# mLSTM cell and squared-ReLU FFN on one core: another order for the main loop's transfers and for the vector work of the first FFN groups

## The chip, the cores and the metric

The kernel runs on one NeuronCore of one Trainium2 chip. The metric is the device time of one launch in microseconds (us); lower is better. PE is the matrix engine (PEld its weight loads), DVE the vector engine, ACT the scalar engine, POOL the GpSimd engine. SP issues nearly all DMAs, strictly in program order: an issue whose wait is not over holds up everything behind it.

## The reference

The first half is an mLSTM cell: batch 4, 8 heads, 768 steps, head size 40. The second half treats its output as 3072 rows of 320 and puts them through a feed-forward network with a squared ReLU.

```python
for t in range(S):
    m_new = np.maximum(f_gate[:, :, t] + m, i_gate[:, :, t])
    f_stab = np.exp(f_gate[:, :, t] + m - m_new)
    i_stab = np.exp(i_gate[:, :, t] - m_new)
    m = m_new
    C = f_stab[:, :, None, None] * C + i_stab[:, :, None, None] * np.einsum('bhd,bhe->bhde', vt, kt)
    n = f_stab[:, :, None] * n + i_stab[:, :, None] * kt
    h_tilde = np.einsum('bhde,bhe->bhd', C, qt)
    nq = np.einsum('bhd,bhd->bh', n, qt)[:, :, None]
    denom = np.maximum(np.abs(nq), 1.0)
    o = 1.0 / (1.0 + np.exp(-o_gate[:, :, t]))
    y[:, :, t] = o * h_tilde / denom
x = y.transpose(0, 2, 1, 3).reshape(3072, 320)
h = np.maximum(x @ w_in, 0.0)          # w_in: 320 x 2048
return h * h @ w_out                   # w_out: 2048 x 320
```

## The kernel before

**Tiling.** The rows are cut into 24 tiles of 128 (tile s: batch s // 6, chunk s % 6). The mLSTM cell is done chunk by chunk: within a chunk as masked scores (`scores`, `weighted`), between chunks through a state C that is decayed and added to. Two tiles make one of 12 FFN groups g. `ffn1_main` and `ffn1_rest` multiply by w_in in four parts per group, `relu_half` (ACT) takes the product out of PSUM (tile h_ps) into r_sb, `square_half` (DVE) squares it into g2. `ffn2_fast` multiplies by w_out in four steps per group, by a scheme with seven products instead of eight for a 2 by 2 block product; `sums` are its DVE additions (tiles S, g), and its `add`s (L759, out of PSUM into y_sb) are DVE work too. y_sb has three buffers for two tiles a group, so one of the group's buffers was the previous group's y1 and is free when that store (L779) has landed.

**Order.** The schedule is written out by hand: each engine gets its instructions in program order and waits on semaphores for the others. So the place of a call in the source sets the place of each of its instructions in the queue of its engine, and of its DMAs in SP's queue.

**The first FFN groups (loop over u = 0 to 7).** Here w_in and w_out are still being fetched and brought to the format that they are used in, piece by piece: `Rounding.words` is two ACT instructions a piece (L195, L197), `Rounding.join` three DVE instructions (L206, L210, L211), one POOL add (L215) and the issue of a later piece's fetch; `step` does what is due of both. Pieces 0 to 9 are w_in. u even: `turn_rows` (PE transposes of a normalised tile, ACT copy), `scores`, a quarter of the FFN's first product, `weighted`, `mask` (POOL, L359) and `weigh` (ACT, L383) of the next tile. u odd: `attend` (PE; then L466 and L471 on DVE, L474 and L479 on POOL), `normalise`, `transposes` of the next tile, another quarter. `idle(n)` issues n bf16 products of zeros that nobody reads; it takes a buffer of the h_ps pool, which has three here, as has the pool of `transposes`, `scores` and `attend`. r_sb has four buffers.

**The main loop (`parts`).** From n = 8 on the groups run in periods of eight parts, r = n % 8: r 0 and 1 are steps 0 and 1 of `ffn2_fast(g)`, r 2 to 5 the four quarters of the first product of group g + 2, r 6 and 7 steps 2 and 3. With b = 7 + 2 * (n // 8), tiles b and b + 1 of the cell are done meanwhile. Data that must be turned goes through DRAM:

- `pair_up(s)` copies k and q of a tile, DRAM to DRAM, into kq_rows (L287, four issues); `load_squares(s)` reads them back as blocks of 32 by 32 into kqT (L309, four issues), and `turn_kq` (DVE, L316) transposes the blocks. Scores on PE (L424) read kqT.
- `store_num(s)` writes the numerators to num_rows (L557), `load_num(s)` reads them back turned (L562, four issues), and `normalise_turned(s)` (DVE, L574 to L583) makes x_sb.
- `store_rows(s)` writes x_sb to x_rows (L613), `load_rows(s)` reads it as blocks (L618, four issues), and `turn_squares(s)` (DVE, L625) makes xT, which the first product (L649, L660) needs for both tiles of its group.

Each read back waits on SP until its write has landed. In a period SP's order is: at r 1 `load_rows(b - 1)`, `pair_up(b + 2)`; at r 2 `load_squares(b + 2)`; at r 3 `store_num(b)`, `load`, `load_num(b)`, `pair_up(b + 3)`; at r 4 `load_A`; at r 5 `store_rows(b)`, `store_num(b + 1)`, `load_rows(b)`, `load_num(b + 1)`; at r 6 y1's store (L779), `load`, `load_o`, `load_squares(b + 3)`; at r 7 y0's store (L784), `load_A`; at the next r 0 `store_rows` of the tile before.

Of the kernel before, what the change touches and what calls it, by code (L numbers as in the profile page):

```python
# [29 lines left out]
def kernel(  # L30
# [200 lines left out]
    rounding = Rounding()  # L231
# [86 lines left out]
    def load_o(s):  # L318
        b, c = divmod(s, NB)
        r, (s0, s1) = next((r, (a, z)) for r, (a, z) in enumerate(RUNS) if a <= s < z)  # L320
        if s == s0:
            st["og", r] = ld.tile([P, 4, H, D], F32, name="og")
        og = st.setdefault(s, {})["og"] = st["og", r][:, s - s0]
        nc.sync.dma_start(og, o_gate[b, :, c * P : (c + 1) * P, :].rearrange("h p d -> p h d"))

    def sigmoid(s):
        nc.scalar.activation(st[s]["og"], st[s]["og"], AF.Sigmoid)
# [28 lines left out]
    def mask(s):  # L356

        A = st[s]["A"][0]
        nc.gpsimd.affine_select(  # L359
            A[:], A[:], compare_op=ALU.is_ge, fill=-1e30, base=0, pattern=[[0, H], [1, P]], channel_multiplier=-1,  # L360
        )
# [55 lines left out]
    def scores(s, o=(False, False)):  # L417
        d = st[s]

        sc = [bank(o[i]) for i in range(2)]  # L420
        for j in range(PR):
            for i in range(2):
                rows = slice(DP * i, DP * i + D)
                nc.tensor.matmul(  # L424
                    sc[i][:, j, :], lhsT=d["kT"][rows, j, :], rhs=d["qT"][rows, j, :], start=True, stop=True,
                )
        d["sc"] = sc

    def weighted(s, spare=False):
        d = st[s]  # L430
        d["P"] = []
        for i in range(2):
            t = ffn.tile([P, W], F32, name="r_sb", bufs=4) if spare else work.tile([P, W], F32, name="P_sb")
            t = t[:].rearrange("p (j t) -> p j t", j=PR)
            d["P"].append(t)
            heads = slice(i, H, 2) if s < KQ_SQ else slice(PR * i, PR * (i + 1))
            nc.vector.tensor_tensor(t, d["sc"][i], d["W"][:, heads, :], op=ALU.mult)  # L437
# [185 lines left out]
    def turn_squares(s):  # L623
        t = st[s]["xT"]
        nc.vector.transpose(t, t)  # L625
        del st[s]
# [38 lines left out]
    def ffn1(g, pp):  # L665
        ffn1_main(g, pp)
        ffn1_rest(g, pp, st["half"][0])

    def relu_half():
        if "half" in st:  # L670
            hs, g4 = st.pop("half")
            rs = []
            for h in hs:
                rs.append(ffn.tile([P, 2, WG], F32, name="r_sb", bufs=4))
                nc.scalar.activation(rs[-1][:], h[:], AF.Relu)  # L675
            st.setdefault("relu", []).append((rs, g4))

    def square_half():
        if st.get("relu"):
            rs, g4 = st["relu"].pop(0)  # L680
            for i, r in enumerate(rs):
                nc.vector.tensor_tensor(g4[:, :, i, :], r[:], r[:], op=ALU.mult)  # L682
# [104 lines left out]
    def do(f, s):  # L787
        if 0 <= s < NT:
            f(s)
# [9 lines left out]
    def idle(n):  # L799
        t = ps_h.tile([P, W], F32, name="idle", tag="h_ps")  # L800
        for _ in range(n):
            nc.tensor.matmul(
                t[:], lhsT=zeros[:, :1].to_broadcast([P, P]), rhs=zeros[:, :1].to_broadcast([P, W]), start=True, stop=True,
            )
# [75 lines left out]
    for u in range(8):  # L880
        s = 2 + u // 2
        relu_half()
        if u % 2 == 0:
            if u == 0:
                ffn1(0, 0)
                scores(s)
                weighted(s)
                relu_half()
                rounding.step()
            else:  # L890
                if u == 2:
                    idle(4)
                turn_rows(s - 1)
                scores(s)
                ffn1(u // 4, u % 4)
            if u == 2:
                rounding.words()
            if u > 0:
                weighted(s)
            if u == 2:  # L900
                mask(s + 1)
                rounding.join()
                rounding.join()
                weigh(s + 1, masked=True)
                rounding.words()
            elif u == 0:
                rounding.words()
                weigh(s + 1, sums=False)
            else:
                weigh(s + 1)  # L910
                square_half()
        else:
            load_A(s + 2)
            for r in {1: (4,), 3: (5, 6), 5: (7,), 7: ()}[u]:
                load(r)
            if u == 5:
                for r in range(4, 8):
                    sigmoid(r)
            attend(s)
            if u == 3:  # L920
                square_half()
            sum_of_h(s)
            if u < 4:
                normalise(s)
            rounding.join()
            if u == 1:
                values(s + 1)
            if u > 4:
                normalise(s)
            for r in {5: (8,), 7: (9,)}.get(u, ()):  # L930
                load(r)
            for r in {5: (7,), 7: (8,)}.get(u, ()):
                pair_up(r)
            if u > 4:
                load_o(2 * s)
                load_o(2 * s + 1)
            transposes(s + 1)
            rounding.words()
            if u == 7:
                ffn1_main(1, 3)  # L940
                turn_rows(5)
                ffn1_rest(1, 3, st["half"][0])
                square_half()
                relu_half()
            else:
                ffn1(u // 4, u % 4)
                if u > 1:
                    square_half()
        if u < 4:
            load_o(4 + u)  # L950
        while rounding.done < NEXT[u]:
            rounding.step()
        if u == 1:
            square_half()
    square_half()
    load_A(8)
    load_squares(7)
# [44 lines left out]
    for n, (which, g, i) in enumerate(parts):  # L1002
        s, at = 6 + n // 4, n % 4

        r, b = (n % 8, 7 + 2 * (n // 8)) if n >= 8 else (None, None)
# [35 lines left out]

        if r == 0 and g > 1:
            sums(g, ALL, (3,))
        elif r == 1 and g > 2:
            do(turn_squares, b - 2)
        elif r == 4:
            do(scale_q, b + 1)
            do(turn_kq, b + 2)
        elif r == 5 and b > 9:
            do(normalise_turned, b)  # L1050
            do(store_rows, b)
        elif r == 7 and g < NG - 1:
            sums(g + 1, ALL, (2,))
# [57 lines left out]
        if r == 0 and g > 1:  # L1111
            do(decays, b + 1)
            do(mask, b + 1)
            square_half()
            do(normalise_turned, b - 1)
            do(store_rows, b - 1)
        elif r == 1:
            if g > 1:
                if g == 2:
                    turn_squares(9)  # L1120
                do(load_rows, b - 1)
                do(pair_up, b + 2)
            square_half()
            if g < NG:
                sums(g, ALL, (4,))
            do(scale_q, b)
            do(turn_kq, b + 1)
        elif r == 2:
            do(masked_W, b + 1)
            do(load_squares, b + 2)  # L1130
            if n == 10:
                load_rows(8)
        elif r == 3:
            do(decays, b + 2)
            do(mask, b + 2)
            attended(b)
            if b % 4 == 3:
                for t in range(b + 1, min(b + 5, NT)):
                    sigmoid(t)
        elif r == 4:  # L1140
            square_half()
            square_half()
            do(masked_W, b + 2)
            do(load_A, b + 3)
            if b > 9:
                do(turn_squares, b - 1)
        elif r == 5:
            do(store_num, b + 1)
            if b > 9:
                do(load_rows, b)  # L1150
                do(load_num, b + 1)
        elif r == 6 and b == 9:
            normalise_turned(9)
            store_rows(9)
            load_num(10)
            load_rows(9)
            load(14)
            turn_squares(8)
        elif r == 7 and b == 9:
            load_o(14)  # L1160
            load_o(15)
            load_squares(12)
            load_A(13)
        elif r == 6:
            do(load, b + 5)
            for t in range(b + 5, min(b + 7, NT)):
                load_o(t)
            do(load_squares, b + 3)
        elif r == 7:
            do(load_A, b + 4)  # L1170
# [35 lines left out]
```

## Time and profile before

| | |
|---|---|
| median of 12 runs | 524.98 us (521.52 to 527.21) |
| the profiled execution's own time | 526.89 us |
| its span, first to last instruction | 525.1 us |
| busy in the span: PE, DVE, ACT, POOL | 512.5, 333.0, 195.0, 88.2 us |
| mean granted clock of PE | 0.994 |
| moved by DMA | 68.06 MB, mean 130 GB/s |

How to read it: in the page's list of 40 slices each digit is the busy share of a slice in tenths; the row PEclk is the clock granted to PE in tenths. In a list of waits a line reads "engine, what waited, line <- what ended the wait: us in total, times, longest us". In a timeline a row is "start us, duration us, engine, line, operation, out<-in, shape, count", with the idle time before it in brackets; SPq rows are DMA issues. In a table of windows each engine has its busy time, then come the granted clock, the DMA share and GB/s.

### The profile page before, as it was taken

What the parts mean: (1) busy time and instruction counts of PE and PEld (TensorE: products, weight loads), DVE (VectorE), ACT (ScalarE), POOL (GpSimd) and SP (SyncE); (2) the same over time, 40 slices, a digit from 0 to 9 for tenths busy, and PEclk for the clock granted to TensorE, in tenths of its full rate; (3) what the DMA queues carried; (4) which work ended last, traced back from release to release, by engine and by line L of the source; (5) the groups of instructions that cost most, each with busy time, mean ns of one, the idle gap of its engine ahead of it and who ended that gap; (6) DMA issues with size and microseconds to landing.
All of it is one profiled execution on the core that took longest, in us unless ns stands there. A gap on an engine that the chain in (4) does not pass through costs nothing. (4 is left out here: it accounts for less than half of the span.)

```text
span 525.1 us, 10345 instructions
## 1 busy us (share of the span) xinstructions
PE 512.5 (98%) x3937; PEld 448.7 (85%) x3937; DVE 333.0 (63%) x638; ACT 195.0 (37%) x460; POOL 88.2 (17%) x110
## 2 busy tenths in 40 slices
PE   9998999999999999899999999989999999999997
PEld 4777888886798988798898898888898898998997
DVE  8479988868884772774774773664865864431451
ACT  3776568452645226232335424233532301102000
POOL 3255643222212010010110010010110100000000
PEclk9899899999999999999999999999999999999999
DMA  9998599876877775875784775775864221200000
GB/s 191 228 198 184 141 194 204 212 170 125 194 139 152 161 144 112 184 126 123 162 140 113 165 134 125 153 144 123 168 151 80 78 73 39 61 12 1 26 27 25
DMA packets 239394, 68.06 MB, mean 130 GB/s; under 512 B 185744, under 2 KB 233872, under 8 KB 239344
## 3 DMA queue, kind: packets, MB, share of 16 engines
q1 hardware_dynamic: 239248, 67.20, 60.6%
q8 instruction: 31, 0.51, 0.4%
q10 hardware_dynamic: 96, 0.20, 0.1%
q14 instruction: 19, 0.16, 0.1%
HBM read 55.08 MB, written 17.86 MB: 139 GB/s over the span
## 5 line engine op out<-in xcount | busy, mean ns | idle before, releaser
L649 PE MATMUL h_ps<-xT,w_in 128*128 128x256 f32 x768 | 174.1, 384 | 5.1 <-DVE xT L625 2.5
L649 PEld LDWEIGHTS h_ps<-xT,w_in 128*128 128x128 f32 x768 | 144.6, 191 | 28.0 <-DVE xT L625 3.4
L675 ACT ACTIVATE r_sb<-h_ps 128x512 f32<-128x512 f32 x96 | 51.4, 598 | 114.7 <-issue 51.5
L743 PE MATMUL h_ps<-w_out,g 128*128 128x160 f32 x528 | 75.5, 299 | 0.0
L682 DVE TENSOR_TENSOR g<-r_sb 128x512 f32<-128x512 f32 x96 | 67.4, 751 | 10.0 <-ACT r_sb L675 10.0
L743 PEld LDWEIGHTS h_ps<-w_out,g 128*128 128x128 f32 x528 | 72.9, 190 | 0.3 <-ACT W_sb L383 0.2
L383 ACT ACTIVATE W_sb<-A_bc,b_T 128x128 f32<-128x128 f32 x176 | 53.8, 388 | 23.4 <-POOL A_bc L359 23.2
L437 DVE TENSOR_TENSOR P_sb<-tp,W_sb 128x512 f32<-128x512 f32 x46 | 29.5, 683 | 44.7 <-PE numT L534 29.9
L743 PE MATMUL h_ps<-T,S 128*128 128x160 f32 x352 | 52.3, 302 | 0.0
L743 PEld LDWEIGHTS h_ps<-T,S 128*128 128x128 f32 x352 | 48.8, 190 | 1.6 <-issue 0.9
L660 PE MATMUL h_ps<-xT,w_in 64*128 64x256 f32 x384 | 49.0, 391 | 0.0
L660 PEld LDWEIGHTS h_ps<-xT,w_in 64*128 64x128 f32 x384 | 34.8, 186 | 12.1 <-issue 8.8
L763 ACT COPY y_sb<-h_ps 128x160 f32<-128x160 f32 x11 | 3.2, 293 | 95.9 <-PE h_ps L743 76.8
L316 DVE STREAM_TRANSPOSE kqT<-kqT 128x1024 f32<-128x1024 f32 x17 | 21.1, 1240 | 26.1 <-DMA kqT<-kq_rows 25.5
L359 POOL TENSOR_SCALAR_AFFINE_SELECT A_bc<-A_bc 128x1024 f32<-128x1024 f32 x22 | 25.4, 1153 | 68.8 <-ACT kq L369 56.7
L759 DVE TENSOR_TENSOR y_sb<-y_sb,h_ps 128x160 f32<-128x160 f32 x44 | 13.9, 315 | 36.0 <-PE h_ps L743 35.9
L396 POOL TENSOR_TENSOR vw<-va,W_sb 128x328 f32<-128x328 f32 x20 | 17.7, 886 | 69.4 <-ACT W_sb L383 50.3
L424 PEld LDWEIGHTS tp<-kqT 40*128 40x128 f32 x384 | 24.9, 188 | 4.8 <-issue 2.7
L490 POOL TENSOR_TENSOR Cd<-C,kq 128x164 f32<-128x164 f32 x15 | 7.0, 464 | 128.8 <-DVE C L551 106.5
L424 PE MATMUL tp<-kqT 40*128 40x128 f32 x384 | 26.5, 276 | 1.7 <-issue 1.2
L743 PE MATMUL h_ps<-w_out,S 128*128 128x160 f32 x176 | 26.0, 301 | 1.4 <-DVE y_sb L759 1.4
L369 ACT ACTIVATE kq<-A_bc 64x512 f32<-64x512 f32 x30 | 18.8, 628 | 21.4 <-DMA A_bc<-a_rows 19.6
(119 smaller groups left out, 602.3 us busy)
## 6 DMA issues: line engine op xcount, KB each, us to landing
A_bc<-a_rows SPq DMA_DIRECT2D x23, 512.0 KB, 5.1
raw<-in_moe_w_out_dram SPq DMA_DIRECT2D x16, 320.0 KB, 3.6
num_rows<-tn SPq DMA_DIRECT2D x18, 256.0 KB, 2.8
kq<-num_rows SPq DMA_DIRECT2D x72, 64.0 KB, 2.2
kqT<-kq_rows SPq DMA_DIRECT2D x34, 128.0 KB, 3.1
raw<-in_moe_w_in_dram SPq DMA_DIRECT2D x8, 512.0 KB, 4.8
kq<-in_k_dram SPq DMA_DIRECT2D x24, 160.0 KB, 4.0
va<-in_v_dram SPq DMA_DIRECT2D x24, 160.0 KB, 4.6
```

Of the source, the lines that this page charges most:

```text
L316: nc.vector.transpose(t, t)
L359: nc.gpsimd.affine_select(A[:], A[:], compare_op=ALU.is_ge, fill=-1e30, base=0, pattern=[[0, H], [1, P]], channel_multiplier=-1,)
L369: nc.scalar.activation(e[rows], st[s]["A"][0][rows, PR * i : PR * (i + 1), :], AF.Exp)
L383: nc.scalar.activation(d["W"][:, i * n + h, :], A[i][:, h, :], AF.Exp, bias=b_T[:, b, c, i * n + h : i * n + h + 1],)
L396: nc.gpsimd.tensor_tensor(d["vw"][:], d["va"][:], d["W"][:, :, P - 1 : P].to_broadcast([P, H, D1]), op=ALU.mult,)
L424: nc.tensor.matmul(sc[i][:, j, :], lhsT=d["kT"][rows, j, :], rhs=d["qT"][rows, j, :], start=True, stop=True,)
L437: nc.vector.tensor_tensor(t, d["sc"][i], d["W"][:, heads, :], op=ALU.mult)
L649: nc.tensor.matmul(hs[i][:, n, :], lhsT=w_in[:, a, fb * P : (fb + 1) * P], rhs=xT[:, :, a, :], start=(n == 0 and a == 0), stop=False,)
L660: nc.tensor.matmul(hs[i][:, n, :], lhsT=w_in2[rows, 2 * pp + n, :], rhs=xT[rows, :, 2, :], start=False, stop=(n == 1),)
L675: nc.scalar.activation(rs[-1][:], h[:], AF.Relu)
L682: nc.vector.tensor_tensor(g4[:, :, i, :], r[:], r[:], op=ALU.mult)
L743: nc.tensor.matmul(to, lhsT=lhsT[:, p], rhs=rhs[:, p, :], start=(start and p == 0), stop=(p == NPAIR - 1), skip_group_check=True,)
```

## The change

In the FFN loop, at u = 1 `relu_half` comes ahead of the steps of the rounding and the `square_half` behind them is left out there. At u = 2 the idle products go; `words`, the mask of the next tile and one `join` come ahead of `weighted`, and the left out `square_half` follows the second `join`. In the main loop `pair_up(b + 2)` goes ahead of `load_rows(b - 1)` at r 1, `load_num(b + 1)` moves from the end of r 5 to r 6, behind y1's store, and `turn_squares(9)` of the second period moves from behind step 1 of `ffn2_fast` to ahead of it.

```diff
             else:
-                if u == 2:
-                    idle(4)
                 turn_rows(s - 1)
                 scores(s)
                 ffn1(u // 4, u % 4)
             if u == 2:
                 rounding.words()
+                mask(s + 1)
+                rounding.join()
             if u > 0:
                 weighted(s)
             if u == 2:
-                mask(s + 1)
                 rounding.join()
-                rounding.join()
+                square_half()
                 weigh(s + 1, masked=True)
                 rounding.words()
...
             load_o(4 + u)
+        if u == 1:
+            relu_half()
         while rounding.done < NEXT[u]:
             rounding.step()
-        if u == 1:
-            square_half()
...
         if r == 0 and g > 1:
             sums(g, ALL, (3,))
-        elif r == 1 and g > 2:
+        elif r == 1 and g > 1:
             do(turn_squares, b - 2)
...
         elif r == 1:
             if g > 1:
-                if g == 2:
-                    turn_squares(9)
+                do(pair_up, b + 2)
                 do(load_rows, b - 1)
-                do(pair_up, b + 2)
             square_half()
...
             do(store_num, b + 1)
             if b > 9:
                 do(load_rows, b)
-                do(load_num, b + 1)
...
         elif r == 6:
+            do(load_num, b + 1)
             do(load, b + 5)
             for t in range(b + 5, min(b + 7, NT)):
                 load_o(t)
```

## The prediction

> **What bounds the kernel now.** I read the page first, then the waits of PE, then the timelines of SP and DVE around each wait.
>
> ```profile
> PE 512.5 (98%) x3937; PEld 448.7 (85%) x3937; DVE 333.0 (63%) x638; ACT 195.0 (37%) x460; POOL 88.2 (17%) x110
> PEclk9899899999999999999999999999999999999999
> ```
>
> PE is busy nearly throughout, and the chain of waits from 353.9 us to the end is PE alone. So only PE's gaps before that can be won, and whatever the change removes or adds there reaches the end undiluted. The waits of PE over 126 to 362 us (four lines), then over 42 to 76 us (two):
>
> ```profile
> PE h_ps L649 <- DVE xT L625: 2.5, 4, 0.9
> PE h_ps L743 <- DVE y_sb L759: 1.4, 3, 0.7
> PE tp L424 <- issue: 1.2, 1, 1.2
> PE tp L424 <- PE h_ps L660: 0.5, 1, 0.5
> ...
> PE h_ps L649 <- ACT r_sb L675: 1.4, 1, 1.4
> PE h_ps L649 <- POOL w_in L215: 0.2, 1, 0.2
> ```
>
> These idle numbers are low, because a modelled end hides part of a wait. I take start to start, against the same pair elsewhere in PE's timeline: L660 to L424 takes 1.84 us undisturbed (252.91 to 254.75), but 3.25 and 2.49 at 211.60 and 331.64. Product to product takes 2.17, but 2.86, 2.55 and 3.05 at 219.64, 259.94 and 338.92. The last product to L649 takes 4.35, but 5.41, 4.83, 4.93 and 5.34 at 187.54, 229.13, 308.06 and 348.59. What is lost: 1.41+0.65, then 0.69+0.38+0.88, then 1.06+0.48+0.58+0.99: 7.1 us in the main loop.
>
> Who causes them is read in SP's timeline (each row is a batch of issues):
>
> ```profile
> 197.87 0.52 SPq L613 DMA_DIRECT2D x_rows<-x_sb  x1
> 202.22 2.19 SPq L618 DMA_DIRECT2D xT<-x_rows  x4
> 204.45 1.79 SPq L287 DMA_DIRECT2D kq_rows<-in_k_dram  x2
> 206.29 1.23 SPq L287 DMA_DIRECT2D kq_rows<-in_q_dram  x2
> 208.63 2.48 SPq L309 DMA_DIRECT2D kqT<-kq_rows  x4
> 211.15 0.65 SPq L557 DMA_DIRECT2D num_rows<-tn  x1
> ...
> 224.17 1.87 SPq L618 DMA_DIRECT2D xT<-x_rows  x4
> 226.14 1.84 SPq L562 DMA_DIRECT2D kq<-num_rows  x4
> 228.07 0.38 SPq L779 DMA_DIRECT2D out_dram<-y_sb  x1
> ```
>
> From 198.39 to 202.22 SP stands still: load_rows (L618) waits for store_rows (L613) to land, and pair_up (L287) stands behind it though it waits for nothing. SP's waits total 27.3 us in nine such stops over 190 to 362 us. DVE shows who pays:
>
> ```profile
> 213.50 1.25 DVE L316 STREAM_TRANSPOSE kqT<-kqT 128x1024 f32<-128x1024 f32 x1 [7.28 <-DMA kqT<-kq_rows]
> 214.67 2.46 DVE L682 TENSOR_TENSOR g<-r_sb 128x512 f32<-128x512 f32 x4
> ...
> 230.17 0.33 DVE L759 TENSOR_TENSOR y_sb<-h_ps,y_sb 128x160 f32<-128x160 f32 x1 [3.66 <-DMA out_dram<-y_sb]
> ```
>
> **The change part by part.**
>
> **pair_up ahead of load_rows (r = 1).** Its four issues take 3.07 us (204.45 to 207.52) and move into the 3.83 us stop, so load_rows still goes out at 202.22. Its last copy would land about 2.4 us after its issue, near 203.9, so load_squares (L309) follows load_rows at 204.4 and not at 208.63: 4.2 us earlier. Its kqT buffer is free (last reader L485, done at 196.26). The squares then land near 209.2 instead of 213.38, and turn_kq (L316) ends near 210.4. The scores that PE wants at 213.44 no longer wait: 1.41 us, and in the same place three groups later 0.65. The four squares (L682) queued behind L316 end near 213, and with them ACT's wait for r_sb. store_num and load_num (landed 217.74) come 4.2 us earlier too, so normalise_turned moves forward, and the y_sb add that PE waits for at 222.50 is no longer at the end of one unbroken DVE run: 0.69 and 0.88. At 259.94 the wait hangs on load_num alone (DVE idles 1.77 us for it): 0.38.
>
> A rule that speaks against this: load_rows itself landed 2.25 to 3.2 us after issue. The Trainium skill, "DMA: Bandwidth & Descriptors", Queues, rings and completion order, has each DMA engine consume descriptors in ring order, so pair_up's data would go first. pair_up's landings are 2.0 us from first to last, so load_rows would land at 209.1 instead of 207.12. turn_squares wants it at 217.04, or about 213 after the change: still nothing lost; with that cover gone it would cost 2.0 us per group.
>
> **load_num behind y1's store (r = 5 to 6).** Four issues (1.84 us) and one store change places. DVE's add into y_sb stands at 230.17, 309.21 and 350.15 only because the old store has not landed; its product on PE ends at 229.3, 308.2 and 348.8. With the store 1.9 us sooner the add is bound by PE. From the add to the end of turn_squares DVE takes 3.73 us (230.17 to 233.90), so it ends at 233.0, 311.9 and 352.5, ahead of PE's need at 233.5, 312.4 and 352.9: 0.48+0.58+0.99. load_num goes 0.5 us later for the store; it landed at 229.51 and is asked for at 231.62, and the edit above brings it earlier. The new risk: SP now waits at L779 for y1's last add, with load_num, load and load_squares behind it. That add ended at 224.01, and SP gets there at 226.04: 2 us of cover, so nothing.
>
> **turn_squares(9) ahead.** One DVE transpose (0.57 us) passes one add. Its rows land at 192.14, PE waits until 192.95: it can gain 0.1 of the 1.06. The passed add is not waited for within 1 us.
>
> Main loop: 1.41+0.65+0.69+0.88+0.38+0.48+0.58+0.99+0.1 = 6.2 us at most. Part may return as another wait, as DMA times scatter: I take 5.6.
>
> **The FFN groups, u = 1 and 2.** idle(4), four bf16 products (1.04 us of PE at 48.09), goes, and relu (two ACT, 1.07 us) passes words, so h_ps is free at 50.1, not 52.3. It buys nothing: the third product instruction needs the weight piece whose join ends on POOL at 52.98, and PE in fact went on at 53.03. Nothing ahead of that join changes on DVE or POOL. The two words (1.2 us of ACT) that relu passes serve the next join, at 53.9.
>
> The waiting has a second price:
>
> ```profile
> 50.50:53.00 2.50, 0.91 (x4) 0.30 (x2) 2.47 (x3) 2.19 (x5) 1.85 (x2) 0.87 1.06 285
> 53.00:55.70 2.70, 2.67 (x6) 2.19 (x7) 2.67 (x4) 1.25 (x2) 1.57 (x2) 0.50 0.59 143
> ```
>
> The granted clock (third from last) is already 0.50 after a wait of 1.43 us. The Trainium skill, "TensorE: Matmul & The Clock Gate", What's actually happening, halves the clock only after an idle window of about 3.4 us and restores it after a busy one. By the rule the longer gap here (about 2.4 us in one piece) costs nothing and even today's slow stretch should not be there: a gain of 1.3. By the trace the slow stretch stays, and if its window is now not busy enough another of 3.4 us at half speed follows: 1.7 lost. I follow the trace and take the same stretch, 0.
>
> Then the order on DVE: now squares, weighted, join, join (53.90 to 61.46); afterwards join, weighted, join, squares. The instructions are the same, but an instruction that meets a running POOL operation stretches: L210 takes 1.37 us instead of 0.43, L211 1.11 instead of 0.69, a square 1.75 instead of 0.68. Today two meet one (+1.1, +0.9). Afterwards join 8 follows join 7 directly, so its L210 meets join 7's POOL add (+1.1) and its L211 the mask (+1.1), and the second square meets join 9's (+1.2): 1.3 us more. attend's L466 starts at 62.7 instead of 61.37; it frees the bank that PE's transposes take at 62.24, so PE waits until 63.2: 0.95. The relu of the third quarter waits for the squares (r_sb) until about 62.7, with 2 us of cover before PE needs that bank. The mask keeps its place on POOL, join's fetches go to SP some 1 us sooner. Later DVE is about 0.8 late against a PE that is 0.95 late: no more. No trace row shows this order: I bound it by -1.3 (clock kept) and +2.7 (both prices), and take +1.0.
>
> Sum: -5.6 + 1.0 = -4.6 us. The profiled execution took 526.89 us (span 525.1 and 1.8 around it): 522.3. It lies 1.9 above the median of the runs, 524.98, which I shift by the same: 520.4.
>
> **The rivals.**
>
> B, the DMA engines are the limit, not SP's order: earlier issues land no earlier. For it: a DMA share near 0.7 in the main loop, and store_rows taking 4 us to land behind a 512 KB load_A. Against it: the squares landed 2.4 to 2.7 us after issue, and SP stands idle. Half of 5.6 stays: -2.8+1.0, 523.2.
>
> C, the FFN groups cost both prices: -5.6+2.7, 522.1. For it, a DVE without idle from 47 to 74 us; against, that a slow PE hides the late DVE.
>
> D, slower: y1's store blocks SP. If DVE's last add of y1 ends after SP has reached L779, load_num waits. load_num takes 3.4 us from first issue to landing and is due about 1.6 us after the add at 229.3, so it hurts from a store later than 227.4 in this trace's time, and each us beyond is paid in six groups: from 1.1 us late (+6.6-5.6+1.0) it is slower, at 1.5 us late 529.4. Against: the add must come 4.5 us later than it does, and the 14.0 us that DVE now idles for the store says the store is what is late.
>
> E, the loop's edits do nothing, since the waits move to load_rows' own landing: only the FFN cost is left, 526.0.
>
> **How the numbers follow.** My forecast 0.68 (all faster), C 0.08 (0.07 faster, 0.01 same), B 0.11 (0.05 and 0.06), E 0.04 (same), D 0.09 (0.01 same, 0.08 slower). 0.3% (1.6 us) is about what a measurement of this kernel can tell from no change: limits 523.4 and 526.6. Faster 0.80, same 0.12, slower 0.08. My forecast's own ends are -6.2-1.3 and -4.5+1.7, that is 517.5 to 522.2; reaching into B for the rest, and leaving the extreme low end out, the range is 517.8 to 524.0.
>
> **What would show it.** Right: in SP's timeline L287 between L613 and L618; L309 some 4 us nearer to L613; L779 ahead of L562; DVE's 14.0 us for out_dram near 2; PE's waits for L759 and at L424 gone, one of about 0.8 for L625 left; near 62 us a new PE wait of 0.5 to 1.5 for DVE L466; the clock still near 0.5 for some 3 us after 53. Wrong: DVE's wait for kqT<-kq_rows as long as now (B), or SP waiting at L779 (D), or PE going on before 53.0.

## The result and the profile after

The changed kernel takes 520.65 us (median of 12 runs, 518.37 to 522.53) against 525.03 us (median of 49, among them those of the table above); the ratio is 0.9917, 95% interval 0.9894 to 0.994, so 4.4 us or 0.8% less. The profiled execution took 518.43 us with a span of 516.6 us, 8.5 us below the span before. That is more than the medians moved, because the two profiled executions lie on opposite sides of their medians. That of before was 1.9 us above: it had a stretch at half clock in its opening (14.8 to 18.2 us), and PE was already 1.9 us behind at the second quarter of the first group, where nothing had been changed yet. That of the changed kernel was 2.2 us below; what sets such executions apart is taken up with the last run. In the comparisons of profiles below, the start of L660 at the second quarter (47.03 us before, 45.17 after) is the zero.

Two lines of the page, then PE's waits over 120 to 355 us (three lines), then those over 42 to 76 us (one):

```profile
PE 508.1 (98%) x3933; PEld 447.2 (87%) x3933; DVE 336.1 (65%) x638; ACT 194.3 (38%) x460; POOL 90.9 (18%) x110
PEclk9999899999999999999999999999999999999999
```

```profile
PE h_ps L743 <- DVE S L738: 0.3, 1, 0.3
PE numT L534 <- DVE P_sb L437: 0.2, 1, 0.2
PE h_ps L649 <- DVE xT L625: 0.2, 1, 0.2
```

```profile
PE h_ps L649 <- POOL w_in L215: 2.6, 2, 2.2
```

All four kinds of wait in the main loop are gone; the 0.2 us for L625 that are left lie at 152 us, ahead of the periods that were edited. At the third quarter PE waits for POOL's add of the seventh weight piece in two pieces of 0.4 and 2.2 us, where it waited for ACT and POOL.

SP's timeline in the period that was shown of before:

```profile
196.65 0.74 SPq L613 DMA_DIRECT2D x_rows<-x_sb  x1
197.44 1.23 SPq L287 DMA_DIRECT2D kq_rows<-in_k_dram  x2
198.71 1.23 SPq L287 DMA_DIRECT2D kq_rows<-in_q_dram  x2
201.10 1.87 SPq L618 DMA_DIRECT2D xT<-x_rows  x4
203.08 3.40 SPq L309 DMA_DIRECT2D kqT<-kq_rows  x4
206.58 0.51 SPq L557 DMA_DIRECT2D num_rows<-tn  x1
...
219.50 1.86 SPq L618 DMA_DIRECT2D xT<-x_rows  x4
221.46 0.41 SPq L779 DMA_DIRECT2D out_dram<-y_sb  x1
221.97 1.82 SPq L562 DMA_DIRECT2D kq<-num_rows  x4
```

pair_up (L287) now fills the time in which store_rows (L613) lands. load_rows (L618) goes out 4.45 us after store_rows, as before (4.35). load_squares (L309) goes out 6.4 us after store_rows instead of 10.8, and y1's store (L779) stands ahead of load_num. DVE's answer:

```profile
209.05 1.25 DVE L316 STREAM_TRANSPOSE kqT<-kqT 128x1024 f32<-128x1024 f32 x1 [4.15 <-DMA kqT<-kq_rows]
210.22 3.00 DVE L682 TENSOR_TENSOR g<-r_sb 128x512 f32<-128x512 f32 x4
...
225.66 0.32 DVE L759 TENSOR_TENSOR y_sb<-h_ps,y_sb 128x160 f32<-128x160 f32 x1 [2.95 <-PE h_ps L743]
```

turn_kq ends at 210.30, 1.8 us before PE wants its scores (212.11), and the add into y_sb is released by PE's product and no longer by a store.

### The profile page after: what moved, and what is told of

It is laid out like the page before. It is cut to its first block, busy times and chain, and to the rows that moved or that the text cites. A ratio compares the mean times of both kernels' runs of the same rounds, so it can differ in the third digit from the quotient of the medians.

```text
span 516.6 us, 10360 instructions
## 1 busy us (share of the span) xinstructions
PE 508.1 (98%) x3933; PEld 447.2 (87%) x3933; DVE 336.1 (65%) x638; ACT 194.3 (38%) x460; POOL 90.9 (18%) x110
## 4 chain that ended last, share of the span: by engine, by line
PE 64%; DVE 0%; issue 0%
PE h_ps L743 29%; PE h_ps L649 22%; PE h_ps L660 6%; PE numT L534 2%; PE tp L424 2%; PE numT L523 1%; PE numT L512 1%; DVE S L738 0%; DVE y_sb L759 0%
## 5 line engine op out<-in xcount | busy, mean ns | idle before, releaser
L675 ACT ACTIVATE r_sb<-h_ps 128x512 f32<-128x512 f32 x96 | 50.3, 599 | 109.2 <-PE h_ps L660 62.5
L682 DVE TENSOR_TENSOR g<-r_sb 128x512 f32<-128x512 f32 x96 | 68.9, 767 | 10.1 <-ACT r_sb L675 10.0
L660 PE MATMUL h_ps<-xT,w_in 64*128 64x256 f32 x384 | 49.0, 391 | 0.0
L660 PEld LDWEIGHTS h_ps<-xT,w_in 64*128 64x128 f32 x384 | 34.8, 186 | 12.1 <-issue 9.1
L759 DVE TENSOR_TENSOR y_sb<-y_sb,h_ps 128x160 f32<-128x160 f32 x44 | 14.1, 320 | 43.5 <-PE h_ps L743 43.5
L359 POOL TENSOR_SCALAR_AFFINE_SELECT A_bc<-A_bc 128x1024 f32<-128x1024 f32 x22 | 26.9, 1221 | 68.2 <-ACT kq L369 53.5
L396 POOL TENSOR_TENSOR vw<-va,W_sb 128x328 f32<-128x328 f32 x20 | 19.1, 956 | 71.3 <-ACT W_sb L383 54.0
L424 PEld LDWEIGHTS tp<-kqT 40*128 40x128 f32 x384 | 24.8, 188 | 2.4 <-issue 0.9
L424 PE MATMUL tp<-kqT 40*128 40x128 f32 x384 | 26.1, 275 | 0.0
```

What stands on the lines that cost most here:

```text
L359: nc.gpsimd.affine_select(A[:], A[:], compare_op=ALU.is_ge, fill=-1e30, base=0, pattern=[[0, H], [1, P]], channel_multiplier=-1,)
L396: nc.gpsimd.tensor_tensor(d["vw"][:], d["va"][:], d["W"][:, :, P - 1 : P].to_broadcast([P, H, D1]), op=ALU.mult,)
L424: nc.tensor.matmul(sc[i][:, j, :], lhsT=d["kT"][rows, j, :], rhs=d["qT"][rows, j, :], start=True, stop=True,)
L660: nc.tensor.matmul(hs[i][:, n, :], lhsT=w_in2[rows, 2 * pp + n, :], rhs=xT[rows, :, 2, :], start=False, stop=(n == 1),)
```

## The experiments

Ratios are against the kernel before, measured beside it on the same chip, with 95% intervals.

**All three edits of the loop, first FFN groups as before.**

```diff
-        elif r == 1 and g > 2:
+        elif r == 1 and g > 1:
...
-                if g == 2:
-                    turn_squares(9)
+                do(pair_up, b + 2)
                 do(load_rows, b - 1)
-                do(pair_up, b + 2)
...
-                do(load_num, b + 1)
...
         elif r == 6:
+            do(load_num, b + 1)
```

> All three edits of the main loop, the first FFN groups as before. My theory (the loop's waits go, the FFN edits cost about 1 us): about 5.5 us below the kernel before, that is 1 us better than the full change; no PE wait of over 0.5 us between 185 and 355 us. Rival 1 (the FFN edits help, as they are meant to): less than the full change gains, at most 4 us below. Rival 2 (the DMA engines are the limit): at most 3 us below, with DVE's waits for kqT and for y_sb's store about as long as before.

Measured: 519.0 us against 525.42, ratio 0.9883 (0.9851 to 0.9916): 6.1 us less. PE's only wait in the loop is 0.2 us for P_sb. Both rivals fall: this is more than the full change gains, and the transfers that were issued earlier did land earlier. Over 120 to 372 us DVE's wait for kqT went from 25.5 to 11.1 us, and that for y_sb's store from 14.0 us to none.

**The FFN edits alone.** The diff is the other half of the change (relu, idle, words, mask, join, squares at u = 1 and 2).

> The edits at u = 1 and 2 alone, the main loop as before. My theory: 1.0 us slower than before (0 to 2.7): PE still goes on only when the POOL add of the seventh weight piece has ended, and then meets DVE 1 us late. Rival (relu was what PE waited for, and the idle products were dead weight): 1 to 2.5 us faster, with PE going on sooner after the second quarter than the 4.9 us that it takes now.

Measured: 526.92 us against 525.42, ratio 1.0035 (1.0015 to 1.0056): 1.8 us slower by the ratio, 1.5 by the medians. So the change is two changes of opposite sign, and -6.1 + 1.8 = -4.3 is the -4.4 of the whole. PE goes on 4.9 us after the end of the second quarter, as it did, so the rival falls.

**pair_up alone, and load_num alone.**

```diff
+                do(pair_up, b + 2)
                 do(load_rows, b - 1)
-                do(pair_up, b + 2)
```

> pair_up ahead of load_rows alone. My theory: the terms 1.41, 0.65, 0.69, 0.88 and 0.38 go, about 4.0 us less than before; the waits of PE for L625 stay (about 2 to 3 us), since y1's store is still behind load_num. Rival (pair_up's data ahead in the rings delays what follows): 1 us or less, with load_rows landing 2 us later than now and DVE's wait for kqT over 15 us.

```diff
-                do(load_num, b + 1)
...
         elif r == 6:
+            do(load_num, b + 1)
```

> load_num behind y1's store alone. My theory: the terms 0.48, 0.58 and 0.99 go, about 2.0 us less than before; DVE's 14 us of waiting for y_sb's store go to about 5 or less; the PE waits at L424 and for L759 stay. Rival (SP now stands at y1's store and load_num comes late instead): no gain or slower, with SP waiting at L779 and DVE waiting for num_rows.

Measured: pair_up alone 520.17 us, ratio 0.9909 (0.9875 to 0.9944), 4.8 us less; load_num alone 523.94 us, 0.9965 (0.9943 to 0.9987), 1.8 us less. PE's waits in the loop, first with pair_up alone (two lines), then with load_num alone (five):

```profile
PE h_ps L649 <- DVE xT L625: 0.9, 1, 0.9
PE numT L534 <- DVE P_sb L437: 0.2, 1, 0.2
```

```profile
PE tp L424 <- PE h_ps L660: 1.5, 2, 0.9
PE h_ps L743 <- DVE y_sb L759: 1.1, 2, 0.7
PE h_ps L649 <- DVE xT L625: 0.9, 1, 0.9
PE h_ps L743 <- ACT y_sb L763: 0.4, 1, 0.4
PE numT L534 <- DVE P_sb L437: 0.2, 1, 0.2
```

The second set is as expected, and DVE's wait for y_sb's store (14.0 us before) is gone with it. The first set is not: moving pair_up took away three of the four waits for L625 too, which I had given to load_num. With the queue some 4 us ahead, load_rows, load_num and y1's store all come early enough even in their old order: here the store is issued at 222.85, against 228.07 (4.0 us sooner, each counted from its zero, which is 45.83 here).

**pair_up and turn_squares(9), without load_num.** The first diff without its last two edits.

> pair_up ahead of load_rows and turn_squares(9) ahead, without the move of load_num, first FFN groups as before. From the profile of pair_up alone, in which PE's waits for L625 at the later groups were gone too: the same as all three edits of the loop, about 6.4 us less than before, so the move of load_num adds nothing where pair_up has moved. Rival (my forecast, which gave load_num's move 2.05 us of its own): about 4.5 us less than before.

Measured: 519.58 us against 525.52, ratio 0.9898 (0.9875 to 0.9921). By the interval both -6.4 and -4.6 us are possible, so times alone do not decide. In the profile the last two of PE's four waits for L625 are gone; at the first the rows were late, and at the second DVE's add still stood 4.9 us for the store (a line of DVE's waits over 120 to 372 us), and PE 1.0 us behind it:

```profile
DVE y_sb L759 <- DMA out_dram<-y_sb: 4.9, 1, 4.9
```

So load_num's move is a safeguard beside pair_up; its worth on average is too small for these intervals to show.

**turn_squares(9) alone.**

> turn_squares(9) ahead of step 1 of the second period alone. The forecast: 0.1 us, since the rows landed only at 192.14 us of the profile before. The other reading, from the profile after: behind the add of step 1, which needs that step's last product, the transpose can never be done before PE asks, so the edit is worth the whole 1.06 us wherever the rows have landed by then: about 1.0 us less, the PE wait for L625 near 192 us gone. Neither can show beyond the noise of a few runs, so the gap at that place in the profile decides.

Measured: ratio 0.9994 (0.9973 to 1.0014). In its profile, DVE's timeline near the place:

```profile
190.72 0.58 DVE L625 STREAM_TRANSPOSE xT<-xT 128x384 f32<-128x384 f32 x1 [0.45 <-DMA xT<-x_rows]
191.22 0.28 DVE L759 TENSOR_TENSOR y_sb<-y_sb,h_ps 128x160 f32<-128x160 f32 x1
```

The transpose passed the add, and then waited for its rows; PE still stood 0.76 us. Both readings hold, one after the other: the rows must have landed (in the full change, the loop's edits alone and, below, the run with DVE's old order they had, or nearly), and the transpose must not stand behind the add (with pair_up alone, 0.9 us were left).

**The idle products kept.**

```diff
             else:
+                if u == 2:
+                    idle(4)
                 turn_rows(s - 1)
```

> The full change, with the four idle products at u = 2 put back. My theory (PE waits there for the POOL add of the seventh weight piece and for nothing else): the same time as the full change within 0.3%, PE going on 4.9 us after the end of the second quarter as before. Rival 1 (removing them costs clock: the array cools down in the longer gap): about 0.5 to 1.7 us faster than the full change, clock above 0.8 in the 3 us after the gap. Rival 2 (they were dead weight): about 1 us slower than the full change.

Measured: 521.76 us, ratio 0.9931 (0.9905 to 0.9957) beside the full change's 0.9917 (0.9894 to 0.994): no difference that can be told. PE goes on 4.9 us after the end of the second quarter here too, so the products stood inside a wait.

**DVE's old order at u = 2, with the rest of the full change.**

```diff
             if u == 2:
                 rounding.words()
                 mask(s + 1)
-                rounding.join()
+                square_half()
             if u > 0:
                 weighted(s)
             if u == 2:
                 rounding.join()
-                square_half()
+                rounding.join()
```

> The full change, but with DVE's old order at u = 2: squares, weighted, join, join (relu ahead and no idle products stay). My theory (the FFN edits cost because DVE reaches attend's L466 about 1 us later): about 1 us faster than the full change, near 519.5, and L466 starting about 14.4 us after the L660 of the second quarter, as before, and not 15.3. Rival (the cost is the clock, or relu ahead of words): the same as the full change.

Measured: 518.5 us against 524.96, ratio 0.9889 (0.9857 to 0.9922), 5.8 us less: as good as the loop alone. What decides is one row of DVE's timeline in four profiles, L466 (before; with the old order here; in the full change; in the full change run again, below):

```profile
61.37 0.49 DVE L466 TENSOR_TENSOR num<-hi,eA_T 128x328 f32<-128x328 f32 x1
```

```profile
59.17 0.49 DVE L466 TENSOR_TENSOR num<-hi,eA_T 128x328 f32<-128x328 f32 x1
```

```profile
60.47 0.48 DVE L466 TENSOR_TENSOR num<-hi,eA_T 128x328 f32<-128x328 f32 x1
```

```profile
61.22 0.48 DVE L466 TENSOR_TENSOR num<-hi,eA_T 128x328 f32<-128x328 f32 x1
```

Their zeros are 47.03, 44.82, 45.17 and 45.92, so L466 starts 14.34, 14.35, 15.30 and 15.30 us after them. With the FFN edits alone it is 15.29: all profiles with DVE's old order and the old joins lie within 0.03 of 14.36, all with the new order within 0.01 of 15.30. The new order costs DVE 0.95 us here. The intervals of this run and of the full change overlap, so it is the median and this row together that speak for the order; that the clock has a part in it too is seen in the last run.

**The joins earlier, in two versions.** The first moves one join ahead of normalise at u = 1 and the squares behind attend's DVE work and behind normalise at u = 3; the second moves three joins and puts turn_rows behind the third quarter. The main lines of the first are these; the comment has what the second puts in their place, and the edits at u = 2 are left out:

```diff
             sum_of_h(s)
+            if u == 1:
+                rounding.join()          # second version: join, join, values, words, join
             if u < 4:
                 normalise(s)
+            if u == 3:
+                square_half()
...
```

> The full change, with the sixth weight piece's join ahead of normalise at u = 1, so that the seventh's ends about 2 us sooner, and both sets of squares of the first two quarters moved behind attend's DVE work and behind normalise. If PE's 2.2 us at the third quarter hang on that join and the FFN cost on L466, both go: 2 to 3.5 us faster than the full change, near 517.5, PE going on about 3 us after the second quarter and not 4.9. Rival (DVE, without idle time from 42 to 74 us, is the bound there, in whatever order its work stands): the wait moves to L466 or to turn_rows, no better than the loop's edits alone, 519 or more.

> The full change, with the joins of pieces 6, 7 and 8 ahead of normalise at u = 1, turn_rows of that tile behind the third quarter on PE, and the squares of the first two quarters behind attend's DVE work and behind normalise at u = 3. If what is left of PE's gap hangs on the seventh piece's join, and L466 is no longer pushed back by squares, PE goes on 2 to 3 us sooner and keeps it: about 2 us better than the loop's edits alone, near 517. Rival (the DVE work up to the next normalise is the bound, whatever its order): a wait for L466 or x_sb takes the place, 518.5 to 519.5.

Measured: 519.14 us, ratio 0.9892 (0.9863 to 0.9921), and 519.44 us, 0.9883 (0.986 to 0.9906). The rival is right in both. PE's waits over 42 to 76 us, the first version (two lines), then the second (three):

```profile
PE tp L633 <- DVE x_sb L602: 1.5, 1, 1.5
PE h_ps L649 <- POOL w_in L215: 0.2, 1, 0.2
```

```profile
PE tp L412 <- DVE num L466: 1.2, 1, 1.2
PE tp L424 <- ACT kqT L415: 1.1, 1, 1.1
PE hi L446 <- DVE P_sb L437: 0.3, 1, 0.3
```

The wait for the weight piece went, or all but 0.2 us of it, and one for what DVE now did later came; in the second version one for ACT came too. In this stretch PE follows DVE.

**load_num later still**, behind load_squares and y0's store.

```diff
         elif r == 6:
-            do(load_num, b + 1)
...
         elif r == 7:
+            do(load_num, b + 1)
             do(load_A, b + 4)
```

> The three edits of the loop, with load_num moved on from r 6 to r 7, behind load_squares and y0's store; first FFN groups as before. It prices the cover of load_num: its issue comes some 9 us later, past the moment (about 5 us after y1's store) when normalise_turned asks for it. If that cover is only about 2 to 4 us, DVE waits for num_rows once a period and PE for L625: 2 to 5 us of PE wait in each of some six periods, 10 to 25 us slower than the loop's edits. If the turned tile has a period of slack after all: no change.

Measured: 547.4 us, ratio 1.0416 (1.0384 to 1.0449). DVE's wait in the second period (its timeline), PE's wait there (its timeline), and that stretch in a table of windows (PE's granted clock is third from last):

```profile
234.85 0.17 DVE L574 TENSOR_SCALAR dm<-kq 128x8 f32<-128x8 f32 x1 [7.19 <-DMA kq<-num_rows]
```

```profile
237.18 10.14 PE L649 MATMUL h_ps<-xT,w_in 128*128 128x256 f32 x32 [6.86 <-DVE xT L625]
```

```profile
236.00:240.00 4.00, 2.82 (x7) 2.26 (x8) 3.97 (x8) 0.00 (x0) 0.00 (x0) 0.50 0.44 121
```

load_num goes out at 231.23, where the loop's edits alone had it at 223.89: some 7 us later. PE stands 6.86 us and then runs its 32 products in 10.1 us instead of 7.2, at half clock for most of that time. So the late transfer costs its delay less the cover, and here 3 us of clock on top. PE's waits for L625 are 19.4 us in four periods, and the whole is 28 us over the loop's edits by the difference of the ratios, above the 10 to 25 expected. That a late load_num is expensive is thus as rival D had it. The change stays clear of it: SP waited at y1's store for 0.2 us in all over 185 to 362 us.

**The full change beside these.**

> The full change itself, beside the three others on one chip, so that the version with the early joins can be held against it: about 4.4 us less than before.

Measured: 520.91 us, ratio 0.9913 (0.9885 to 0.9941). Its profile has no stretch at half clock after the gap at the third quarter (clock 1.00 over 51 to 54.5 us), and PE waits 1.78 us for L466 instead; in the profile after there was the stretch, and a wait of 0.26. Both arrive at the third tile's turn_rows (L633) 21.38 us after the zero. At that place the half clock costs nothing: it is spent in the time in which DVE is awaited anyway.

Behind the wait for L466 it is not hidden. The profile with the idle products kept has the same wait of 1.78 us, and a granted clock of 0.50 from 61.0 to 67.8 us. PE's two rows behind that wait, in this run and then in that one:

```profile
61.76 1.09 PE L412 MATMUL tp<-ident,kq 128*128 128x128 f32 x8 [1.78 <-DVE num L466]
62.69 3.62 PE L649 MATMUL h_ps<-xT,w_in 128*128 128x256 f32 x16
```

```profile
62.10 1.97 PE L412 MATMUL tp<-ident,kq 128*128 128x128 f32 x8 [1.78 <-DVE num L466]
63.86 5.57 PE L649 MATMUL h_ps<-xT,w_in 128*128 128x256 f32 x16
```

PE arrives at L633 24.16 us after its zero there, 2.8 us later than here, and that execution took 522.07 us against 519.25.

How often this matters is seen in the single executions, since each has its mean granted clock on record (number of executions and their mean time):

| | clock above 0.995 | clock below 0.995 |
|---|---|---|
| full change (12 and these 6) | 7, 519.0 us | 11, 521.7 us |
| idle products kept | 5, 518.5 us | 10, 522.0 us |
| FFN edits alone | 10, 525.6 us | 12, 528.1 us |
| DVE's old order | 4, 518.2 us | 2, 520.5 us |
| the loop's edits alone | 5, 519.2 us | 1, 519.2 us |
| before, beside these runs | 59, 524.8 us | 23, 526.0 us |

So a good part of what the FFN edits cost is that more executions spend more time at half clock. Above 0.995 they cost 0.8 us without the loop's edits (525.6 against 524.8 for the executions of before beside them), and with them nothing that shows (519.0 and 518.5 against 519.2, from different comparisons).

The best versions are the loop's edits without the FFN edits, and the full change with DVE's old order. By the intervals they cannot be told from each other, nor from the full change with certainty; their medians, 519.0 and 518.5, are 1.6 to 2.4 us below the two of the full change.

## Why the prediction was right

- **The total.** 520.4 was forecast, 520.65 measured. The two sums behind it: 5.6 less for the loop, 6.1 measured (4.4 to 7.8 by the interval); 1.0 more for the FFN edits, 1.8 measured (0.8 to 2.9). That the total is closer than either part is luck: the loop gave 0.5 us more than forecast, the FFN edits took 0.8 more, and the two errors cancel.
- **pair_up.** Each step came out: it fits into the time in which SP stood, load_rows was issued only 0.1 us later, load_squares came 4.3 us nearer to store_rows (4.2 forecast), and the waits at L424 and for L759 went. Ring order, which was feared at 2.0 us, took 0.25 at most: load_rows had landed 9.5 us after store_rows was issued, against 9.25. pair_up's four copies landed within 0.6 us of each other, right behind store_rows. One reading was off without effect: of load_rows' four issues before, the third took 3.83 us to land, not at most 3.2.
- **load_num: the step that was mis-attributed.** I gave its move 2.05 us of its own. Alone it has them (1.8), but beside pair_up they were mostly won already. The terms of the sum overlapped: I treated waits of one queue as independent, though every stop taken out moves all that follows in that queue. The sum held because the same microseconds were counted only once, though under the wrong edit.
- **turn_squares(9): the term that was mis-sized.** 0.1 us was right for rows that land at 192.14. In the full change they landed earlier against PE, and the whole 1.06 us went. I took one execution's landing for a fixed time.
- **relu and the idle products.** Worth nothing, as forecast: PE went on 6.0 us after the zero by either order, at the end of the same POOL add.
- **DVE's order.** The mechanism was right: L466 came 0.95 us later, where I had 1.3. The term that was too large is the stretching: I had 1.1, 1.1 and 1.2 us for join 8's L210, its L211 and the second square; in the profile after they stretched by 0.94 (to 1.37), 0.77 (to 1.46) and 1.08, and join 9's L206 by 0.16. For L210 the prediction's own figures (1.37 instead of 0.43) had given 0.94. PE's own delay at that place was 0.63 us in the profile after, 0.37 from the clock and a wait of 0.26, where I had a wait of 0.95 and no clock term.
- **The clock: a term put at 0 that is not.** I followed the trace and took the same stretch at half clock behind the gap at the third quarter. There it is a matter of the execution: it followed the gap in four of seven profiles with the first FFN groups as before, and in three of five with relu ahead of words. It is hidden there too: the profile after, which has it, and that of the last run, which has not, reach L633 at the same time, so my -1.3 was worth nothing. The +1.7 was half right. A further stretch does come in more executions, but in the one profile that shows it, it stands behind the wait for L466 and not behind this gap, and it costs 2.8 us and not 1.7. Rival C, with both prices and 522.1, is thus near the slower 11 of the 18 executions (521.7 on average), and the median of 520.65 lies between the two groups.
- **What stays open.** Why the FFN edits bring the further stretch is argued and not shown: the wait for L466 is 1.78 us with the new order and 0.86 with the old in the profiles without a stretch ahead of it, and where the stretches of the executions without a profile lie is not known. In the profiles of the full change PE also loses up to 0.3 us each at 152 and 185 us, waiting for DVE; that DVE carries its delay so far was not tried by itself.

## What to carry to other kernels

In a queue that issues in order, look for issues that wait for nothing behind one that waits for a landing. Moving them into that gap cost nothing here, and it brought everything behind them forward, well beyond the wait that it was meant for. When several edits act on one queue, do not add up their waits: take one out and redo the rest. Where an engine has no idle time over a stretch, the order of its work decided which wait showed on the others; what would shorten the stretch is less work, or less collision with its neighbour. And before a profile is read as the kernel, see where its execution stands among the others: here two groups of executions lie 2.7 us apart, and the profile after came from the faster one.

## What the runs showed of the hardware

- DVE instructions that meet POOL operations stretch in a repeatable way: L210 takes 1.37 or 1.38 us instead of 0.43 where it follows another join directly, and L211 1.46 instead of 0.69 beside the mask. Through this the order of the same instructions moves L466 by 0.95 us, the same to within 0.04 over twelve profiles.
- PE's granted clock fell to half behind short gaps, in some executions and not in others with the same gap: at the third quarter, behind waits of 1.4 to 2.2 us, in 7 of 12 profiles; behind a wait of 0.86 us for L466 in the profile of the loop's edits alone, not in those of pair_up alone and of turn_squares(9) alone; behind one of 1.78 us with the idle products kept, not in the full change run again. The prediction cites a rule by which half clock comes only after about 3.4 us of idleness; these runs do not bear it out as a limit. The stretches lasted 3.4 us or a multiple of it: 3.41 in the profile after, 6.83 with the idle products kept, 10.24 behind the gap of 6.9 us with load_num late.
- Four DRAM to DRAM copies issued ahead of a load in the same queue moved its last landing by 0.25 us only in the period shown (from 9.25 to 9.5 us after the store's issue).
